# v in two fp16 parts, and gelu and norms in attention with other steps, in an adaLN block of attention and two MLPs

## The chip, the cores and the metric

The kernel runs on one core of one Trainium2 chip. Its time is the device time of one execution in microseconds (us). Before the change the median of three runs is 2027.78 us (2027.35 to 2031.98). A core has engines that work side by side, each through its own instructions in a fixed order: PE (matmul; its weight loads are listed apart as PEld), DVE (vector), ACT (scalar, with functions such as exp and tanh), POOL, and SP, which issues all DMAs here. Matmuls write PSUM, which has 8 banks; POOL works in SBUF only in this kernel.

## The reference, cut to what matters

```python
mod = (silu(c) @ w_mod).reshape(..., 6, 1, -1)
sa, ca, ga, sb, cb, gb = (mod[:, i] for i in range(6))
h = layernorm(x) * (1 + ca) + sa
x = x + ga * attention(h, wqkv, wo)        # 32 heads of 16, softmax over 2048 keys
h = layernorm(x) * (1 + cb) + sb
x = x + gb * mlp(h, w1, w2, w3, w4)

def mlp(x, w1, w2, w3, w4):
    h = gelu(layernorm(x) @ w1)            # tanh form
    hs = shifted(h) @ w2                   # each quarter of the columns moved by +1, -1, +2, -2 rows
    x1 = x + hs
    return x1 + gelu(layernorm(x1) @ w3) @ w4
```

x is 2048 x 512 in fp32, w3 is 512 x 1792. Products other than those with P are made of three matmuls of a high and a low part of each factor.

## The kernel before

Attention goes over 4 chunks of 512 queries and, in each, over 16 pairs of heads: 64 units of 16 steps (128 keys each). A step has two `sc` matmuls (scores, keys by queries, one per head) whose bank ACT turns into P with an exp (L982), and two `mb` matmuls (L970) for a unit that comes later, of which DVE takes the maximum over keys (L966) as the softmax's shift. PE may write a bank again when the exp or the maximum has read it; seven banks are shared by `sc`, `mb` and all other matmuls beside attention, of which those may own three, and one bank holds `pv`.

The exp writes P as an int32 whose upper 16 bits are read as one fp16 number and whose lower 16 bits are the rest. The lower half is turned into fp16 in place, times 0.5, by POOL for a whole step (L1034) or by ACT in two instructions (line 1034's other branch, listed as L123), whichever the planner expects to be done sooner. `pv_part` multiplies both halves with v (L1060 upper half, L1057 lower half). v is kept in DRAM (`Vs`), 192 two-byte numbers per key and pair of heads: three bf16 parts for the upper half, scaled with a constant for the sum of P, and one fp16 part for the lower half. `v_tiles` makes them in chunk 0: two copies on ACT, the rest on DVE, its copy on ACT (L743), the second rest on POOL (L744). After a unit, ACT copies `pv` to `ac` (L1078), PE transposes it, DVE adds the parts (L1096), and POOL divides by the sum.

Beside attention's chunk 0 run the projections and the splitting of weights (`pieces_gen`, with L868 and L869). Beside chunks 1 to 3 run the tails of chunks 0 to 2: wo, the residual, two norms, w1 with gelu, the shift, w2, a norm, w3 with gelu, w4. The rest of the third tail and the whole fourth come after attention, with all 8 banks. A norm's first step in `tail` runs on DVE: centred and times `cbrow` (L1319), times the deviation's inverse plus `sbrow` (L1322). A gelu (`gelu`) beside attention is a chain: ACT square (L1352) and copy (L1353) of the bank, DVE cube (L1357), which frees the bank, ACT tanh (L1361), ACT halving (L1362), POOL product (L1363), ACT high part (L1347), POOL low part (L1348). After attention it is: ACT halved copy (L1366) and square (L1340), which frees the bank, then cube (L1367), tanh (L1368), product (L1369, on DVE), high and low part.

The order is made when the program is built. A planner (`Sched`) keeps a time for each engine by assumed costs; chains wait in a list, and `misc` puts their next step into an engine's order where it expects it not to delay attention's own. `fill` puts matmuls of the projections and tails between blocks of three rows of `sc` and `mb`, with a budget for each step (`SC0`, `TAILB`). The chip then runs each engine in that order and waits on semaphores.

Of the kernel before, what the change touches and what calls it, by code (L numbers as in the profile page):

```python
# [33 lines left out]
VHI = 2.0 ** 39  # L34
VMAX = 2.0 ** 14
VD = 20

SC0 = (32, 900.0, 700.0)
TAILB = (0.0, 500.0, 500.0, 540.0)
# [245 lines left out]
def cA(n=CH):  # L285
    return n / 1.2 + 52
# [11 lines left out]
def kernel(ctx, tc, A_x, A_wqkv, A_wo, B_w1, B_w2, B_w3, B_w4, c, w_mod, out):  # L298
# [45 lines left out]
    def v_hi(t):  # L344
        return t[:, :, 0:128].rearrange("p a (b n) -> p a b n", b=2)
# [205 lines left out]
    def bounds():  # L551
        yield lambda: ("mod", 0) in done and ("mod", 1) in done

        def g():
            dve.scalar_tensor_tensor(gcol, modcol, -1.0, modcol, op0=OP.mult, op1=OP.max)
            dve.scalar_tensor_tensor(gcol[:, 0:4], gcol[:, 4:8], D ** 0.5, gcol[:, 0:4], op0=OP.mult, op1=OP.add)
            dve.tensor_scalar(gcol[:, 0:4], gcol[:, 0:4], 1.0 / (VMAX * VHI), None, op0=OP.mult)
        sch.chain(("D", 250, g), mark("gb"))
# [148 lines left out]
    def v_tiles(w, a, kts):  # L707
        wh, wl = halves(w, KT)
        for kt in kts:
# [13 lines left out]
            r = qp.tile([P, H // 4, 2, DH], F32, name="vr", tag="vr", bufs=2)  # L723

            def rest(v=v, b3=b3, r=r, b=b):
                dve.tensor_tensor(r, b3, v[:, :, :, 0:DH], op=OP.subtract)
# [13 lines left out]
            sch.chain(("A", cA(256), lambda v=v, b3=b3: act.activation(v[:, :, :, 0:DH], b3, AF.Copy)),  # L740
                      ("A", cA(256), lambda vl=vl, b3=b3: act.activation(vl[:, :, :, 8:8 + DH], b3, AF.Copy, scale=1.0 / VHI)),
                      ("D", cD(256), rest),
                      ("A", cA(256), lambda v=v, r=r: act.activation(v[:, :, :, VD:VD + DH], r, AF.Copy)),  # L743
                      ("G", cG(256), lambda v=v, r=r: pool.tensor_tensor(v[:, :, :, 2 * VD:2 * VD + DH], r, v[:, :, :, VD:VD + DH],  # L744
                                                                         op=OP.subtract)),
                      (None, 0, store), prio=VP, bank=b)

    def v_weights(a):
# [94 lines left out]
    def pieces_gen():  # L843
        while True:
# [23 lines left out]
            sch.chain(*ops, ("A", cA(), lambda f=f, w=w: act.activation(w, f, AF.Copy)),  # L868
                      ("G", cG(), lambda f=f, t=t, w=w: pool.tensor_tensor(t, f, w, op=OP.subtract)),  # L869
# [152 lines left out]
    def p_low(s):  # L1022

        p = pt[s].rearrange("p j n -> p (j n)")
        o, i = p.bitcast(F16)[:, 0::2], p.bitcast(U16)[:, 0::2]
        ready = e_exp.pop(s) + XX
        g, a = [max(sch.T[e], ready) for e in "GA"]
        if g > a + LACT:

            for h in range(2):  # L1030
                c = slice(h * CH, (h + 1) * CH)
                e_low[s] = XP["A"] + sch.crit("A", 690, ready, partial(act.activation, o[:, c], i[:, c], AF.Copy, scale=0.5))
        else:
            e_low[s] = XP["G"] + sch.crit("G", 1345, ready, lambda: pool.tensor_scalar(  # L1034
                o, i, 0.5, 1.0, op0=OP.mult, op1=OP.mult))
# [5 lines left out]
    def pv_part(s, lo):  # L1041
# [8 lines left out]
        def mms():  # L1050
            for j in range(2):
                for i in range(2):
                    r = 64 * j + 32 * i
                    if lo:
                        n = 9 + DH if i else 1 + DH
                        c = 128 + 32 * j + 9 + DH
                        te.matmul(acc[r:r + n, :], v[:, (kt + i) % 4, c - n:c].bitcast(F16), pt[s + i].bitcast(F16)[:, j, 0::2],  # L1057
                                  start=False, stop=kt == NKT - 2, skip_group_check=True)
                    else:
                        te.matmul(acc[r:r + 32, :], v[:, kt % 4, r:r + 32], pt[s].bitcast(F16)[:, j, 1::2],  # L1060
# [21 lines left out]
    def o_fin(u, ac, ready):  # L1082
# [12 lines left out]
        def sums():  # L1095
            dve.reduce_sum(sm, bv[:, :, 0:3 * VD].rearrange("p th (a d) -> p th d a", a=3)[:, :, 0:DH + 1, :], axis=AX.X)  # L1096
# [9 lines left out]
        sch.chain(("D", 490, sums), ("D", 90, lambda: dve.reciprocal(rc, sm[:, :, DH:DH + 1])), ("G", 350, fin),  # L1106
# [86 lines left out]
    def tail(ci):  # L1193
# [107 lines left out]
        for i, t in enumerate(new):  # L1301
# [13 lines left out]
            r, m, ops = ln_ops(x1, True)  # L1315
# [8 lines left out]
            go = partial(sch.chain, ("D", cD(), x1_add), ops[0], ("D", cD(), center), ops[1], ("D", cD(), scale), *ops2,  # L1324
# [9 lines left out]
        def gelu(b, n, hi, lo, key):  # L1334
# [4 lines left out]
            def square():  # L1339
                act.activation(sq, b, AF.Square)  # L1340
                sch.free(b)

            def end():
# [3 lines left out]
            tail_ops = (("A", cA(n), lambda: act.activation(hi, xs, AF.Copy)),  # L1347
                        ("G", cG(n), lambda: pool.tensor_tensor(lo, xs, hi, op=OP.subtract)), (None, 0, end))  # L1348
            if psd["s"]:

                def square_copy():
                    act.activation(sq, b, AF.Square)  # L1352
                    act.activation(xs, b, AF.Copy)  # L1353
                    sch.T["A"] += cA(n)

                def cube():
                    dve.scalar_tensor_tensor(sq, sq, 1.0 / GELU_A, b, op0=OP.add, op1=OP.mult)  # L1357
                    sch.free(b)

                sch.chain(("A", cA(n), square_copy), ("D", cD(n), cube),  # L1360
                          ("A", cA(n), lambda: act.activation(sq, sq, AF.Tanh, scale=GELU_A * GELU_C)),  # L1361
                          ("A", cA(n), lambda: act.activation(sq, sq, AF.Copy, scale=0.5, bias=0.5)),  # L1362
                          ("G", cG(n), lambda: pool.tensor_tensor(xs, xs, sq, op=OP.mult)), *tail_ops, bank=b)  # L1363
                return

            sch.chain(("A", cA(n), lambda: act.activation(xs, b, AF.Copy, scale=0.5)), ("A", cA(n), square),  # L1366
                      ("D", cD(n), lambda: dve.scalar_tensor_tensor(sq, sq, 1.0 / GELU_A, xs, op0=OP.add, op1=OP.mult)),  # L1367
                      ("A", cA(n), lambda: act.activation(sq, sq, AF.Tanh, scale=2.0 * GELU_A * GELU_C)),  # L1368
                      ("D", cD(n), lambda: dve.scalar_tensor_tensor(xs, sq, 1.0, xs, op0=OP.add, op1=OP.mult)),  # L1369
                      *tail_ops, bank=b)  # L1370
# [242 lines left out]
```

## Time and profile before

| | |
|---|---|
| median of three runs | 2027.78 us |
| profiled execution | 2035.15 us |
| its span, first to last instruction | 2033.4 us |
| granted PE clock, mean | 0.98 |
| first `sc` matmul | 100.1 us |
| end of attention's chunk 0 | 556.5 us |
| last copy out of `pv` | 1861.3 us |
| exps (L982) | 2048, 1084.1 us busy |
| maxima (L966) | 2048, 1275.7 us busy |
| lower halves of P on POOL (L1034) | 973, 1294.3 us busy |

A group's row names line, engine, operation, tile written and tile read, sizes and count; behind the bar its busy time in us and the mean duration in ns; behind the next bar the idle time of its engine just before its instructions, and what ended that idle time. A row of waits names who waited, for whom, the total in us, how many times, and the longest. PE's busy time holds the whole way of a matmul through the array, so a busy PE is not always one that takes new columns.

### The profile page before, as it was taken

To read this page: it belongs to the slowest core of one execution; us is meant where nothing else is said; L and a number is where in the kernel's file an instruction comes from. 1 tells how busy PE (TensorE), PEld (TensorE's weight loads), DVE (VectorE), ACT (ScalarE), POOL (GpSimd) and SP (SyncE) were. 2 spreads that over 40 slices of the span, in tenths; PEclk is the share of its full clock that TensorE was granted. 3 is DMA by queue.
4 is the path that set the end of the run, shared out by engine and by line. 5 is a ranking of instruction groups with operands and counts; after the bars stand their busy time and mean duration, and the time that the engine had idled before them with its cause. 6 is when DMAs were issued, how large, how long until landed. Compare 5 with 4: busy or idle time off the path is not lost.

```text
span 2033.4 us, 41682 instructions
## 1 busy us (share of the span) xinstructions
PE 1931.8 (95%) x14464; PEld 1151.1 (57%) x14464; DVE 1638.4 (81%) x2936; ACT 1528.8 (75%) x3332; POOL 1700.9 (84%) x1653
## 2 busy tenths in 40 slices
PE   6989999999999999999989999999999999999899
PEld 4655555555454555555445555555555555556788
DVE  8879887687899888788998888788898888872644
ACT  5366887778867987787869897787778888796443
POOL 5378899889988998999889998898889998897532
PEclk8999999999998999999999999999999999999899
DMA  5664578876643334434523433333533233434332
GB/s 188 193 199 145 169 215 248 267 230 229 194 146 113 113 109 128 128 119 149 156 86 92 133 113 109 102 118 122 161 109 106 88 113 113 154 93 153 150 125 89
DMA packets 230619, 293.20 MB, mean 144 GB/s; under 512 B 123636, under 2 KB 175348, under 8 KB 214120
## 3 DMA queue, kind: packets, MB, share of 16 engines
q1 hardware_dynamic: 230408, 290.53, 45.5%
q8 instruction: 115, 1.88, 0.4%
q14 instruction: 96, 0.79, 0.1%
HBM read 226.49 MB, written 62.91 MB: 142 GB/s over the span
## 4 chain that ended last, share of the span: by engine, by line
PE 58%; DVE 16%; ACT 14%; POOL 5%; DMA 3%; issue 3%; SPq 1%; POOLq 0%; DVEq 0%; ACTq 0%
PE mb L970 12%; DVE mx L966 9%; PE pv L1060 9%; PE sc L986 8%; ACT pt L982 8%; PE w L326 6%; PE w L328 5%; PE w L330 5%; PE pv L1057 4%; POOL pt L1034 3%; ACT pt L123 1%; PE ot L1089 1%; SPq L102 1%; ACT sq L1352 1%; DVE tst L337 1%
## 5 line engine op out<-in xcount | busy, mean ns | idle before, releaser
L1034 POOL TENSOR_SCALAR pt<-pt 128x1024 f16<-128x1024 uint16 x973 | 1294.3, 1367 | 117.3 <-ACT pt L982 114.9
L966 DVE TENSOR_REDUCE mx<-mb 128x1 f32<-128x512 f32 x2048 | 1275.7, 682 | 112.5 <-PE mb L970 87.1
L982 ACT ACTIVATE pt<-sc 128x512 int32<-128x512 f32 x2048 | 1084.1, 614 | 235.1 <-PE mb L970 185.5
L970 PE MATMUL mb<-kst,qtl 64*128 64x512 f32 x2048 | 758.0, 454 | 56.0 <-ACT pt L982 23.2
L986 PE MATMUL sc<-qtl,kst 64*128 64x512 f32 x2048 | 721.2, 445 | 7.5 <-ACT pt L982 1.8
L970 PEld LDWEIGHTS mb<-kst,qtl 64*128 64x128 f32 x2048 | 348.9, 193 | 266.0 <-ACT pt L982 101.2
L986 PEld LDWEIGHTS sc<-qtl,kst 64*128 64x128 f32 x2048 | 335.6, 186 | 163.5 <-DVE mx L966 49.4
L1060 PE MATMUL pv<-pt,vst 128*32 128x512 f16 x4096 | 360.0, 399 | 3.2 <-DMA vst<-Vs 3.2
L1057 PE MATMUL pv<-pt,vst 128*17 128x512 f16 (+1 forms) x2048 | 211.6, 394 | 1.8 <-POOL pt L1034 1.3
L1060 PEld LDWEIGHTS <-vst 128*32 128x32 bf16 x4096 | 91.3, 95 | 168.8 <-issue 107.7
L326 PE MATMUL w<-A,wr 128*128 128x256 f32 (+2 forms) x576 | 177.6, 308 | 1.6 <-ACT A L320 1.4
L1348 POOL TENSOR_TENSOR g<-xs,g 128x256 fp32r<-128x256 f32 (+2 forms) x144 | 104.2, 724 | 84.9 <-ACT g L1347 84.8
L328 PE MATMUL w<-A,wr 128*128 128x256 f32 (+2 forms) x576 | 170.8, 297 | 1.0 <-DVE A L316 0.7
L330 PE MATMUL w<-A,wr 128*128 128x256 f32 (+2 forms) x576 | 168.9, 293 | 0.0
L326 PEld LDWEIGHTS w<-A,wr 128*128 128x128 f32 x576 | 111.2, 193 | 33.2 <-DVE mx L966 11.2
L326 PE MATMUL w<-wr,g 128*128 128x512 f32 x288 | 118.9, 413 | 0.9 <-ACT g L1347 0.9
L328 PEld LDWEIGHTS w<-A,wr 128*128 128x128 f32 x576 | 111.4, 193 | 12.8 <-issue 10.5
L330 PEld LDWEIGHTS w<-A,wr 128*128 128x128 f32 x576 | 111.4, 193 | 6.5 <-issue 6.5
L330 PE MATMUL w<-wr,g 128*128 128x512 f32 x288 | 113.7, 395 | 0.3 <-POOL g L1348 0.3
L328 PE MATMUL w<-wr,g 128*128 128x512 f32 x288 | 113.6, 395 | 0.0
L1450 DVE TENSOR_TENSOR x<-x,w 128x512 f32<-128x512 f32 x64 | 44.0, 687 | 84.5 <-PE w L330 84.2
L1357 DVE SCALAR_TENSOR_TENSOR sq<-sq,w 128x256 f32<-128x256 f32 (+1 forms) x108 | 43.3, 401 | 64.5 <-ACT xs L1353 60.4
(148 smaller groups left out, 2250.7 us busy)
## 6 DMA issues: line engine op xcount, KB each, us to landing
wr<-Ws SPq DMA_DIRECT2D x80, 1024.0 KB
vst<-Vs SPq DMA_DIRECT2D x256, 192.0 KB
kst<-Ks SPq DMA_DIRECT2D x189, 256.0 KB
qtl<-Qs SPq DMA_DIRECT2D x192, 64.0 KB
Vs<-vt SPq DMA_DIRECT2D x32, 384.0 KB
Ws<-wq SPq DMA_DIRECT2D x40, 256.0 KB
Ws<-wst SPq DMA_DIRECT2D x40, 256.0 KB
wst<-in_B_w_dram SPq DMA_DIRECT2D x36, 256.0 KB
```

The lines of the kernel that those rows point to most:

```text
L326: te.matmul(o, lh, rh, start=first, stop=False)
L328: te.matmul(o, lh, rl, start=False, stop=False)
L330: te.matmul(o, ll, rh, start=False, stop=last)
L966: end = sch.crit("D", 605, e + PX, lambda: dve.reduce_max(mxs[u][:, j, g, c:c + 1], b, axis=AX.X))
L970: return ready, lambda: te.matmul(b, lhs, kst[u % 3][r, c * CH:(c + 1) * CH], start=True, stop=True), after
L982: ea = sch.crit("A", 480, e + PX, lambda: act.activation(pt[s][:, j], b, AF.Exp))
L986: return ready, lambda: te.matmul(b, kst[u % 3][r, kt * P:(kt + 1) * P], qst[u][r], start=True, stop=True), after
L1034: e_low[s] = XP["G"] + sch.crit("G", 1345, ready, lambda: pool.tensor_scalar(o, i, 0.5, 1.0, op0=OP.mult, op1=OP.mult))
L1057: te.matmul(acc[r:r + n, :], v[:, (kt + i) % 4, c - n:c].bitcast(F16), pt[s + i].bitcast(F16)[:, j, 0::2], start=False, stop=kt == NKT - 2 ...
L1060: te.matmul(acc[r:r + 32, :], v[:, kt % 4, r:r + 32], pt[s].bitcast(F16)[:, j, 1::2], start=kt == 0, stop=False, skip_group_check=True)
L1348: ("G", cG(n), lambda: pool.tensor_tensor(lo, xs, hi, op=OP.subtract)), (None, 0, end))
L1450: dve.tensor_tensor(x1, x1, b, op=OP.add)
```

## The change

- v is kept as two fp16 parts for the upper half of P, and one fp16 part, scaled, for the lower half. The third part's two steps (L743, L744) go; DVE writes the second part itself. The ones that make the sum of P change their constant, and the lower half of P is multiplied by 2^-22 instead of 0.5. DVE adds two parts instead of three (136 x 2 numbers instead of 136 x 3). All lower-half matmuls have 17 columns of weights, of which half had 25. `Vs` keeps its size.
- A gelu has one form in all places: ACT square, DVE cube, ACT tanh, DVE product, ACT high part, POOL low part. Cube and product both read the bank, which is free after the product. The factor 0.5 goes into w2 and w4 (18 ACT instructions when they are split).
- Four norms in each of the first three tails go another way: ACT applies mean and deviation (L1281), POOL multiplies with `cbrow` and adds `sbrow` (L1330, L1331).
- Nine of the 40 low parts of split weights go from POOL to DVE (in pieces of wo and w4).
- `TAILB`, the planner's budget of filling work per step, is 560 in the third and fourth chunk instead of 500 and 540.

```diff
-VHI = 2.0 ** 39
-VMAX = 2.0 ** 14
-VD = 20
+VMAX = 2.0 ** 15
+VONE = 2.0 ** 8
+PLOW = 2.0 ** -22
+VLOW = 2.0 ** -40 / PLOW
...
-TAILB = (0.0, 500.0, 500.0, 540.0)
+TAILB = (0.0, 500.0, 560.0, 560.0)
...
             def rest(v=v, b3=b3, r=r, b=b):
-                dve.tensor_tensor(r, b3, v[:, :, :, 0:DH], op=OP.subtract)
+                dve.tensor_tensor(v[:, :, :, 1, 0:DH], b3, v[:, :, :, 0, 0:DH], op=OP.subtract)
                 sch.free(b)
...
                       ("D", cD(256), rest),
-                      ("A", cA(256), lambda v=v, r=r: act.activation(v[:, :, :, VD:VD + DH], r, AF.Copy)),
-                      ("G", cG(256), lambda v=v, r=r: pool.tensor_tensor(v[:, :, :, 2 * VD:2 * VD + DH], r, v[:, :, :, VD:VD + DH],
-                                                                         op=OP.subtract)),
                       (None, 0, store), prio=VP, bank=b)
...
+            if nm in ("w2", "w4"):
+                ops.append(("A", cA(), lambda f=f: act.activation(f, f, AF.Copy, scale=0.5)))
             sch.chain(*ops, ("A", cA(), lambda f=f, w=w: act.activation(w, f, AF.Copy)),
+                      ("D", 2 * cD(), lambda f=f, t=t, w=w: dve.tensor_tensor(t, f, w, op=OP.subtract)) if nm in rows and c else
                       ("G", cG(), lambda f=f, t=t, w=w: pool.tensor_tensor(t, f, w, op=OP.subtract)),
...
             e_low[s] = XP["G"] + sch.crit("G", 1345, ready, lambda: pool.tensor_scalar(
-                o, i, 0.5, 1.0, op0=OP.mult, op1=OP.mult))
+                o, i, PLOW, 1.0, op0=OP.mult, op1=OP.mult))
...
-            dve.reduce_sum(sm, bv[:, :, 0:3 * VD].rearrange("p th (a d) -> p th d a", a=3)[:, :, 0:DH + 1, :], axis=AX.X)
+            dve.reduce_sum(sm, bv.rearrange("p th (a d) -> p th d a", a=2)[:, :, 0:DH + 1, :], axis=AX.X)
...
-            r, m, ops = ln_ops(x1, True)
+            way = not end and i in (0, 1, 2, 3)
+            if way:
+                r, ops = ln_ops(x1)
+                m = None
+            else:
+                r, m, ops = ln_ops(x1, True)
...
+            if way:
+                norm = (*ops, ln_apply(xb, x1, r), ("G", cG(), lambda xb=xb: pool.tensor_tensor(xb, xb, cbrow, op=OP.mult)),
+                        ("G", cG(), lambda xb=xb: pool.tensor_tensor(xb, xb, sbrow, op=OP.add)))
+            else:
+                norm = (ops[0], ("D", cD(), center), ops[1], ("D", cD(), scale))
...
+            def cube():
+                dve.scalar_tensor_tensor(sq, sq, 1.0 / GELU_A, b, op0=OP.add, op1=OP.mult)
+
+            def prod():
+                dve.scalar_tensor_tensor(xs, sq, 1.0, b, op0=OP.add, op1=OP.mult)
+                sch.free(b)
+
+            sch.chain(("A", cA(n), lambda: act.activation(sq, b, AF.Square)), ("D", cD(n), cube),
+                      ("A", cA(n), lambda: act.activation(sq, sq, AF.Tanh, scale=GELU_A * GELU_C)),
+                      ("D", cD(n), prod),
+                      ("A", cA(n), lambda: act.activation(hi, xs, AF.Copy)),
+                      ("G", cG(n), lambda: pool.tensor_tensor(lo, xs, hi, op=OP.subtract)), (None, 0, end), bank=b)
```

The planner makes a new order from it. The built programs count: lower halves of P on POOL 973 before and 999 now, ACT instructions for them 102 and 50 (70 and 38 while the planner is in chunks 1 to 3, 30 and 12 in chunk 0). PE has 14384 matmuls in both; 854 stand after the last `pv` matmul before, 869 now.

Three places show how the order moves. The first is ACT in the tail of chunk 0, a gelu of w1 (`w_10733` before, `w_10579` now, is its bank; `pt<-sc` rows are exps). Before:

```order
L1352 ACTIVATE sq<-w_10733 128x256
L1353 ACTIVATE xs<-w_10733 128x256
L982 ACTIVATE pt_612<-sc 128x512
L982 ACTIVATE pt_613<-sc 128x512 x2
L1361 ACTIVATE sq<-sq 128x256
L1362 ACTIVATE sq<-sq 128x256
L982 ACTIVATE pt_614<-sc 128x512 x2
L982 ACTIVATE pt_615<-sc 128x512 x2
L982 ACTIVATE pt_608<-sc 128x512 x2
L1347 ACTIVATE g_10732<-xs 128x256
```

Now, up to the same high part:

```order
L1360 ACTIVATE sq<-w_10579 128x256
L982 ACTIVATE pt_602<-sc 128x512
L982 ACTIVATE pt_603<-sc 128x512 x2
L1361 ACTIVATE sq<-sq 128x256
L1078 ACTIVATE ac<-pv 128x512
L982 ACTIVATE pt_604<-sc 128x512 x2
L1363 ACTIVATE g_10578<-xs 128x256
```

The copy behind the square and the halving behind the tanh are gone, and the high part comes after two exps instead of six.

The second place is DVE at the same gelu; `mx<-mb` rows are maxima. Before:

```order
L966 TENSOR_REDUCE mx<-mb 128x1 x7
L1357 SCALAR_TENSOR_TENSOR sq<-sq,w_10733 128x256
L966 TENSOR_REDUCE mx<-mb 128x1 x8
L1016 TENSOR_REDUCE mf<-mx 128x8
L966 TENSOR_REDUCE mx<-mb 128x1 x3
```

Now, with the next gelu's two rows behind it:

```order
L1354 SCALAR_TENSOR_TENSOR sq<-sq,w_10579 128x256
L966 TENSOR_REDUCE mx<-mb 128x1 x2
L1357 SCALAR_TENSOR_TENSOR xs<-sq,w_10579 128x256
L966 TENSOR_REDUCE mx<-mb 128x1 x4
L1354 SCALAR_TENSOR_TENSOR sq<-sq,w_10703 128x256
L966 TENSOR_REDUCE mx<-mb 128x1 x2
L1357 SCALAR_TENSOR_TENSOR xs<-sq,w_10703 128x256
```

The product (now L1357) stands two maxima behind its cube (now L1354), as it does in 87 of the 108 gelus beside attention.

The third place is POOL at the first norms of the first tail; `pt<-pt` rows are lower halves of P, `trs` rows the deviation's inverse and what is made of it, one column each. Before:

```order
L1034 TENSOR_SCALAR pt_611<-pt_611 128x1024
L1270 TENSOR_TENSOR trs<-tmv,mhalf 128x1
L1034 TENSOR_SCALAR pt_612<-pt_612 128x1024
L1034 TENSOR_SCALAR pt_613<-pt_613 128x1024
L1034 TENSOR_SCALAR pt_614<-pt_614 128x1024
```

Now:

```order
L1270 TENSOR_TENSOR trs<-tmv,mhalf 128x1
L1274 TENSOR_TENSOR trs<-tmv,trs 128x1
L1275 TENSOR_SCALAR trs<-trs 128x1
L1034 TENSOR_SCALAR pt_604<-pt_604 128x1024
L1330 TENSOR_TENSOR xb<-xb,cbrow 128x512
L1331 TENSOR_TENSOR xb<-xb,sbrow 128x512
L1034 TENSOR_SCALAR pt_605<-pt_605 128x1024
```

Two products over 512 columns stand between two lower halves of P, and two more one-column steps behind the first.

More of the change, by code (lines that the diff above doesn't have):

```diff
@@ L344, in v_hi @@
     def v_hi(t):
[L345 removed]
+        return t[:, :, 0:128].bitcast(F16).rearrange("p a (b i n) -> p a b i n", b=2, i=2)
     def v_lo(t):
@@ L1104, in fin @@
                 sch.add(tail(ci))
-        sch.chain(("D", 490, sums), ("D", 90, lambda: dve.reciprocal(rc, sm[:, :, DH:DH + 1])), ("G", 350, fin),
+        sch.chain(("D", 350, sums), ("D", 90, lambda: dve.reciprocal(rc, sm[:, :, DH:DH + 1])), ("G", 350, fin),
                   *([mark(("att", ci))] if pr == NP - 1 else []), prio=0, bank=b)
@@ L1345, in end @@
                 live.remove(key)
[L1347 to L1370, printed above, removed]
+            def cube():
[8 more added lines that the diff above has]
+                      ("G", cG(n), lambda: pool.tensor_tensor(lo, xs, hi, op=OP.subtract)), (None, 0, end), bank=b)
         def wait_bank():
```

30 lines of the change are left out of this document (13 added, 17 removed).

## The prediction

> **What bounds the kernel now.** I read the page's busy shares and chain first, then the window view cut where the trace shows the first score matmul (100.1), the end of attention's first chunk (556.5) and the last copy out of `pv` (1861.3).
>
> ```profile
> PE 1931.8 (95%) x14464; PEld 1151.1 (57%) x14464; DVE 1638.4 (81%) x2936; ACT 1528.8 (75%) x3332; POOL 1700.9 (84%) x1653
> ...
> PE 58%; DVE 16%; ACT 14%; POOL 5%; DMA 3%; issue 3%; SPq 1%; POOLq 0%; DVEq 0%; ACTq 0%
> ```
> ```profile
> core 0: us, PE busy (x) PEld busy (x) DVE busy (x) ACT busy (x) POOL busy (x), PEclk, DMA share, GB/s
> 0.00:100.10 100.10, 80.27 (x371) 56.41 (x371) 81.13 (x160) 42.78 (x83) 45.41 (x62) 0.90 0.60 188
> 100.10:556.50 456.40, 434.73 (x3267) 243.71 (x3267) 366.22 (x638) 352.66 (x728) 409.45 (x351) 0.97 0.69 211
> 556.50:1861.30 1304.80, 1259.30 (x9981) 712.70 (x9980) 1099.49 (x1967) 1059.27 (x2341) 1184.48 (x1154) 0.99 0.38 118
> 1861.30:2033.40 172.10, 157.53 (x851) 138.23 (x849) 91.56 (x172) 74.13 (x182) 61.56 (x89) 0.96 0.37 137
> ```
>
> Call the four stretches A, B (chunk 0, with the v and q/k projections beside it), C (chunks 1 to 3, with three tails) and D (the rest). In C no engine is alone the bound: PE is busy 97%, POOL 91%, DVE 84%, ACT 81%, all in fixed orders that wait on each other. The groups of C show who holds PE:
>
> ```profile
> L1034 POOL TENSOR_SCALAR pt<-pt 128x1024 f16<-128x1024 uint16 x736 | 978.8, 1366 | 86.4 <-ACT pt L982 84.6
> L966 DVE TENSOR_REDUCE mx<-mb 128x1 f32<-128x512 f32 x1490 | 928.9, 682 | 64.3 <-PE mb L970 51.5 <-PE sc L986 7.9
> L982 ACT ACTIVATE pt<-sc 128x512 int32<-128x512 f32 x1538 | 816.5, 615 | 190.8 <-PE mb L970 149.9 <-PE sc L986 36.8 <-POOL pt L1034 1.7
> L970 PE MATMUL mb<-kst,qtl 64*128 64x512 f32 x1489 | 549.0, 451 | 39.9 <-ACT pt L982 16.6 <-DVE mx L966 6.1 <-DVE sq L1357 5.8
> ...
> L970 PEld LDWEIGHTS mb<-kst,qtl 64*128 64x128 f32 x1488 | 254.2, 193 | 187.8 <-ACT pt L982 72.4 <-DVE mx L966 51.3 <-issue 15.3
> ...
> L986 PEld LDWEIGHTS sc<-qtl,kst 64*128 64x128 f32 x1536 | 249.3, 185 | 118.6 <-ACT pt L982 34.9 <-DVE mx L966 32.6 <-issue 18.2
> ```
>
> PE waits 72.4 + 34.9 + 16.6 = 123.9 us for exps that free a bank, and 51.3 + 32.6 = 83.9 us for maxima that do. A weight load's wait is not all lost, since earlier matmuls still run: before the `mb` matmuls PE itself idles 39.9 us where their loads idle 187.8, 21%. That ratio and 1 are the two ends below.
>
> **The change, stretch C.** 106 of the 108 gelus of the run that stand in attention are here.
>
> ```profile
> L1363 POOL TENSOR_TENSOR xs<-xs,sq 128x256 f32<-128x256 f32 (+1 forms) x108 | 76.1, 705 | 12.7 <-ACT sq L1362 11.7
> ...
> L1362 ACT ACTIVATE sq<-sq 128x256 f32<-128x256 f32 (+1 forms) x108 | 46.8, 433 | 1.6
> ...
> L1357 DVE SCALAR_TENSOR_TENSOR sq<-sq,w 128x256 f32<-128x256 f32 (+1 forms) x108 | 43.3, 401 | 64.5 <-ACT xs L1353 60.4 <-POOL pt L1034 3.7 <-POOL trs L1270 0.2
> ...
> L1353 ACT ACTIVATE xs<-w 128x256 f32<-128x256 f32 (+1 forms) x108 | 41.8, 387 | 0.0
> ```
> ```profile
> L123 ACT ACTIVATE pt<-pt 128x512 f16<-128x512 uint16 x72 | 51.9, 808 | 0.0
> ...
> L1418 POOL TENSOR_TENSOR xb<-xb,gbrow 128x512 f32<-128x512 f32 x11 | 14.2, 1293 | 0.0
> ...
> L1322 DVE SCALAR_TENSOR_TENSOR xb<-xb,trs,sbrow 128x512 f32<-128x512 f32 x12 | 12.9, 1073 | 0.0
> ...
> L1319 DVE SCALAR_TENSOR_TENSOR xb<-x,tmv,cbrow 128x512 f32<-128x512 f32 x12 | 10.4, 864 | 0.0
> ```
> ```profile
> L1281 ACT ACTIVATE xn<-xb,trs 128x512 f32<-128x512 f32 x32 | 26.2, 818 | 29.3 <-POOL trs L1275 29.3
> ...
> L1275 POOL TENSOR_SCALAR trs<-trs 128x1 f32<-128x1 f32 x32 | 6.6, 207 | 2.8
> ...
> L1096 DVE TENSOR_REDUCE sm<-ot 128x136 f32<-128x408 f32 x64 | 36.8, 575 | 5.8 <-PE ot L1089 5.8
> ```
>
> - ACT loses the copy (41.0 us for 106) and the halving (45.9). By the changed order 34 of the 72 half-P conversions leave it (51.9 / 72 = 0.72 us, 24.5). It gains 12 norm applies like L1281 (9.8). Sum **-101.6 us**. ACT's work beside the exps is 1059.3 - 816.5 = 242.8, so 42% of it goes.
> - DVE gains a second product per gelu, which reads the bank as L1357 does: +42.5. It loses 12 norms' two steps (-23.3) and a third of the elements in 48 sums (at most 192 ns each; I take 7 us in all). Sum **+12**, 7% of its 170.6 us beside the maxima.
> - POOL loses L1363 (-74), gains 17 conversions of 1.33 us (978.8 / 736; +22.6), 24 products like L1418 (+31) and 24 one-column steps (+5). Sum **-15**.
> - PE's instruction counts stay. The parts of v are fp16 instead of bf16, stationary at 32 columns for the upper half of P and 17 (half of them 25 before) for the lower; I price that at nothing, since the bf16 and the fp16 kind differ by 1% here:
>
> ```profile
> L1060 PE MATMUL pv<-pt,vst 128*32 128x512 f16 x4096 | 360.0, 399 | 3.2 <-DMA vst<-Vs 3.2
> ...
> L1057 PE MATMUL pv<-pt,vst 128*17 128x512 f16 (+1 forms) x2048 | 211.6, 394 | 1.8 <-POOL pt L1034 1.3
> ```
>
> The new product's price hangs on its operands. In D the cube reads a copy in SBUF, and so does the product:
>
> ```profile
> L1369 DVE SCALAR_TENSOR_TENSOR xs<-sq,xs 128x256 f32<-128x256 f32 x22 | 12.6, 571 | 10.4 <-ACT sq L1368 9.9 <-POOL g L1348 0.6
> ...
> L1322 DVE SCALAR_TENSOR_TENSOR xb<-xb,trs,sbrow 128x512 f32<-128x512 f32 x4 | 3.0, 743 | 0.0
> ```
>
> With two SBUF operands the product takes 571 ns, with one in the bank 401 (L1357, some of its tiles smaller); and the same norm step takes 743 ns in D but 1073 in C, where POOL is busier. I take 401 and keep 571 as the upper end, +18 us of DVE. [...]
>
> **From engine time to span in C.** If PE's waits for exps shrink with what ACT does besides, 42% of 123.9 is -52 us. Waits for DVE grow, with these rows:
>
> ```profile
> DVE sq L1357 <- ACT xs L1353: 56.5, 63, 6.8
> ...
> PEld w L326 <- DVE mx L966: 16.7, 44, 0.5
> ...
> PEld mb L970 <- DVE sq L1357: 13.0, 19, 1.2
> ```
>
> 7% of 83.9 + 16.7 is +7, and a second DVE step per gelu doubles the 13.0. That leaves -32 if all of it is lost time, -7 at the 21%; the middle is -19. A wait goes and one comes: the cube no longer waits out ACT's copy (0.39 us, 63 times, -24 us of DVE idling), but the product waits for the tanh, with the maxima queued behind it, which free PE's banks. The new order puts two maxima (1.36 us) between cube and product; a tanh is about as long as the removed L1362 (0.43). So the new wait lies between 0 and the old 56.5; I let the two nearly cancel and take -3. C: **-22**.
>
> **Stretch B.**
>
> ```profile
> L982 ACT ACTIVATE pt<-sc 128x512 int32<-128x512 f32 x510 | 267.6, 612 | 44.3 <-PE mb L970 35.6 <-PE sc L986 5.5 <-POOL pt L1034 2.6
> ...
> L970 PEld LDWEIGHTS mb<-kst,qtl 64*128 64x128 f32 x513 | 89.2, 194 | 71.1 <-ACT pt L982 28.8 <-DVE mx L966 21.7 <-issue 5.5
> ...
> L869 POOL TENSOR_TENSOR wst<-wst,wq 128x512 fp32r<-128x512 f32 x40 | 51.8, 1301 | 3.9 <-ACT wq L868 3.9
> ...
> L868 ACT ACTIVATE wq<-wst 128x512 fp32r<-128x512 f32 x40 | 25.8, 644 | 6.8 <-POOL wst L857 3.8 <-DMA Ws<-wq 3.0
> ...
> L744 POOL TENSOR_TENSOR vt<-vr,vt 128x256 bf16<-128x256 f32 x22 | 16.1, 737 | 13.1 <-ACT vt L743 13.1
> ...
> L426 DVE TENSOR_TENSOR wp<-wst,wp 128x512 fp32r<-128x512 f32 x10 | 10.6, 1067 | 0.0
> ...
> L743 ACT ACTIVATE vt<-vr 128x256 bf16<-128x256 f32 x21 | 9.3, 451 | 1.6 <-DVE vr L726 1.6
> ```
>
> ACT: -9.3, 18 conversions fewer (30 to 12 in the order, -13), 18 halvings of w2 and w4 more (+11.6): -11, 13% of its 85 us beside the exps. DVE: nine weight remainders from POOL, at L426's 1.07 us +10, sums -2. POOL: -16.1 - 11.7 + 9 x 1.33 = -16, while it is the busiest at 90%. The PE waits that ACT frees (13% of 28.8) and those that DVE adds are under 5 us each and cancel; the end set by POOL is -16 / 0.9 = -18, the other end +6. I take **-3**.
>
> **Stretches A and D.** Ten of the 32 v tiles (L744 has 22 in B) fall into A, where their two removed steps run beside PE's projections and the store to `Vs` keeps its size: 0; the end is the 10 x 0.73 us of POOL work, -7. D's order has 15 matmuls more behind the last `pv` (869 for 854); at 157.53 / 851 = 0.185 us, +2.8. That is also all that the larger `TAILB` budgets amount to in the end, and they shift filling matmuls between the steps of C only. In D the gelu loses its copy:
>
> ```profile
> L1366 ACT ACTIVATE xs<-w 128x256 f32<-128x256 f32 (+1 forms) x36 | 15.0, 417 | 43.4 <-PE w L330 42.6 <-POOL g L1348 0.5
> ```
>
> ACT is idle more than half of D and PE stops only 14.6 us, so I give -1.8 of the 15.0. D: **+1**. Together -22 - 3 + 1 = **-24 us**. The profiled execution took 2035.15 (span 2033.4 and 1.75 around it), 7.4 above the median of the three runs, so I subtract from both alike: 2011 profiled, **2004** as median.
>
> **Rivals.**
> - PE is the bound, and ACT only idles more. For: 97% busy, and exps already wait 149.9 us for `mb`. Against: those waits end where banks are freed by ACT. Price: the 21% end, -7 in C, 0 in B, +1 to +2.8 in D: about -5, 2023.
> - All the freed time counts. C -32 with DVE's -24 added in part, B -18: about -50, 1978. For: POOL, the fullest but PE, loses work as well. Against: DVE gains 12.
> - Slower: the product stalls DVE at its place behind the tanh, and maxima behind it keep banks from PE. If it waits like the cube did (56.5 / 63 = 0.9 us) on half to all of 106, that is 48 to 95 us; half of it lost at PE, less the 24 gained, is 0 to +24 (2028 to 2052); from a mean wait of 0.45 us on all of them nothing is left of the gain. The bank, which the gelu holds until the product, is late at the same place. For: the product sits in DVE's fixed order, and PE already waits 13.0 us behind the cube. Against: ACT, which makes the tanh late, has 102 us less to do. I price it at 2050.
> - POOL, with 17 conversions more and the norms, stalls `pv`: its sum is still -15, so I fold this into the first.
>
> **Chances.** Forecast (1988 to 2016) 0.49; deeper 0.15; PE-bound (2016 to 2034) 0.20; slower 0.16. A measurement tells from no change about 0.3%, 6 us. Faster takes the first two and 0.06 of the third: 0.70; same 0.13; slower 0.17. The range 1976 to 2038 takes in all but 0.05 below and 0.13 above.
>
> **What would show it.** Right: in C, ACT near 958 busy, DVE near 1110, POOL near 1170, the weight loads' waits for `pt` L982 well under 107 us, C some 1283 long. Wrong: DVE's product idling over 45 us behind the tanh; or PE's waits for ACT gone and C as long, which is the PE-bound case; or D longer than 175.

## The result and the profile after

| | before | after |
|---|---|---|
| median of five runs, us | 2027.78 (2026.82 to 2032.26) | 2080.09 (2074.76 to 2081.40) |
| profiled execution: span, us | 2033.4 | 2078.3 |
| granted PE clock, mean | 0.98 | 0.98 |

The changed kernel takes 1.0233 times as long (95% interval 1.0218 to 1.0248), some 47 us more by that ratio (the medians of the table differ by 52), where the prediction had 24 less. The page of the changed kernel, busy shares and then the chain by engine and by line:

```profile
PE 1941.8 (93%) x14464; PEld 1156.6 (56%) x14464; DVE 1646.4 (79%) x3029; ACT 1452.2 (70%) x3026; POOL 1726.5 (83%) x1578
...
PE 53%; POOL 17%; DVE 14%; ACT 7%; issue 4%; DMA 3%; SPq 1%; POOLq 0%; ACTq 0%; DVEq 0%
POOL pt L1034 13%; PE mb L970 11%; DVE mx L966 8%; PE sc L986 8%; PE pv L1060 7%; PE w L327 6%; PE w L331 5%; PE w L329 5%; ACT pt L982 4%; PE pv L1057 4%; DMA vst<-Vs 1%; SPq L103 1%; PE ot L1089 1%; DVE sq L1354 1%; DVE xs L1357 1%
```

ACT's share of the chain fell from 14% to 7%. But POOL's rose from 5% to 17%, and 13% is one line: L1034, the conversion of the lower half of P. The busy share of POOL does not show it, 83% after 84%.

The window view of the changed kernel, cut at the same events as in the prediction (first `sc` matmul 99.8, end of chunk 0 562.7, last copy out of `pv` 1904.9), with the same columns:

```profile
0.00:99.80 99.80, 78.54 (x392) 56.88 (x392) 81.43 (x161) 40.06 (x77) 38.12 (x51) 0.91 0.63 193
99.80:562.70 462.90, 432.90 (x3249) 241.70 (x3248) 369.70 (x645) 341.71 (x699) 407.07 (x324) 0.97 0.66 203
562.70:1904.90 1342.20, 1272.62 (x9962) 719.00 (x9959) 1109.18 (x2047) 1006.15 (x2108) 1221.99 (x1118) 0.98 0.37 117
1904.90:2078.30 173.40, 157.75 (x869) 139.02 (x869) 86.07 (x178) 64.33 (x146) 59.31 (x86) 0.97 0.36 135
```

Against before A is 0.3 us shorter, B 6.5 longer, C 37.4 longer and D 1.3 longer: 44.9 in the span, nearly all of it where POOL converts P. DVE (1109) is where the prediction had it (near 1110); POOL is 52 us over its 1170.

How a group tells this apart from more work. The row of all conversions, first of the kernel before, then of the changed one with the matmuls that read what it writes:

```profile
L1034 POOL TENSOR_SCALAR pt<-pt 128x1024 f16<-128x1024 uint16 x973 | 1294.3, 1367 | 117.3 <-ACT pt L982 114.9
```
```profile
L1034 POOL TENSOR_SCALAR pt<-pt 128x1024 f16<-128x1024 uint16 x999 | 1360.3, 1362 | 146.1 <-ACT pt L982 70.0
...
L1057 PE MATMUL pv<-pt,vst 128*17 128x512 f16 x2048 | 227.1, 394 | 28.2 <-POOL pt L1034 27.7
```

One conversion lasts as long as before (1362 and 1367 ns). But 973 times 1367 ns is 1330 us and the busy time 1294: the conversions lay over each other or over a neighbour by 36 us. 999 times 1362 ns is 1360.6, the busy time to 0.3 us: now nothing overlaps. And of the idle time ahead of a conversion all but 2.4 us had a releaser before; now 146.1 - 70.0 = 76 us have none, 76 ns for each. They are gaps of about 79 ns, one ahead of most conversions, too short for the rows to name what ended them. The matmuls behind it, which stood 1.3 us for L1034, stand 27.7.

The timeline shows the seams themselves (start, duration; a row of x3 is three in a run). The kernel before:

```profile
999.14 3.92 POOL L1034 TENSOR_SCALAR pt<-pt 128x1024 f16<-128x1024 uint16 x3
...
1003.17 1.33 POOL L1034 TENSOR_SCALAR pt<-pt 128x1024 f16<-128x1024 uint16 x1
1004.45 0.39 POOL L1100 TENSOR_TENSOR osb<-sm,rc 128x128 f32<-128x128 f32 x1
```

The changed kernel, some 25 us later:

```profile
1027.90 1.35 POOL L1034 TENSOR_SCALAR pt<-pt 128x1024 f16<-128x1024 uint16 x1
1029.33 0.20 POOL L1019 TENSOR_TENSOR nm<-mf,nm 128x8 fp32r<-128x8 f32 x1
1029.49 0.41 POOL L1100 TENSOR_TENSOR osb<-sm,rc 128x128 f32<-128x128 f32 x1
1029.98 9.93 POOL L1034 TENSOR_SCALAR pt<-pt 128x1024 f16<-128x1024 uint16 x7
```

Before, L1100 starts at 1004.45 while the conversion ahead of it runs to 1004.50. After, L1019 starts 0.08 us behind a conversion's end (1027.90 + 1.35 = 1029.25), and the next conversion 0.08 behind L1100's end; between L1019 and L1100 there is an overlap as ever (0.04 us). Three conversions in a run took 3.92 us, one each (3.92 - 1.36) / 2 = 1.28; seven now take 9.93, one each 1.43. Over the whole traces the median from start to start of two conversions that follow directly, less than 1.7 us apart, is 1289 ns (522 pairs) and 1437 ns (640 pairs): **148 ns more each**, with their duration unchanged. What changed in this instruction is one number: the factor, 0.5 before and 2^-22 now.

### The profile page after: what moved, and what is told of

Same layout as the page of the kernel before. It is cut to its first block, busy times and chain, and to the rows that moved or that the text cites. A ratio compares the mean times of both kernels' runs of the same rounds, so it can differ in the third digit from the quotient of the medians.

```text
span 2078.3 us, 42310 instructions
## 1 busy us (share of the span) xinstructions
PE 1941.8 (93%) x14464; PEld 1156.6 (56%) x14464; DVE 1646.4 (79%) x3029; ACT 1452.2 (70%) x3026; POOL 1726.5 (83%) x1578
## 4 chain that ended last, share of the span: by engine, by line
PE 53%; POOL 17%; DVE 14%; ACT 7%; issue 4%; DMA 3%; SPq 1%; POOLq 0%; ACTq 0%; DVEq 0%
POOL pt L1034 13%; PE mb L970 11%; DVE mx L966 8%; PE sc L986 8%; PE pv L1060 7%; PE w L327 6%; PE w L331 5%; PE w L329 5%; ACT pt L982 4%; PE pv L1057 4%; DMA vst<-Vs 1%; SPq L103 1%; PE ot L1089 1%; DVE sq L1354 1%; DVE xs L1357 1%
## 5 line engine op out<-in xcount | busy, mean ns | idle before, releaser
L1034 POOL TENSOR_SCALAR pt<-pt 128x1024 f16<-128x1024 uint16 x999 | 1360.3, 1362 | 146.1 <-ACT pt L982 70.0
L1057 PE MATMUL pv<-pt,vst 128*17 128x512 f16 x2048 | 227.1, 394 | 28.2 <-POOL pt L1034 27.7
L1060 PEld LDWEIGHTS <-vst 128*32 128x32 f16 x4096 | 91.5, 95 | 173.3 <-issue 110.5
L327 PE MATMUL w<-A,wr 128*128 128x256 f32 (+2 forms) x576 | 176.2, 306 | 0.3 <-ACT A L321 0.3
L327 PEld LDWEIGHTS w<-A,wr 128*128 128x128 f32 x576 | 110.0, 191 | 34.2 <-issue 10.5
L327 PE MATMUL w<-wr,g 128*128 128x512 f32 x288 | 119.2, 414 | 1.9 <-DVE xs L1357 1.9
L1057 PEld LDWEIGHTS <-vst 128*17 128x17 f16 x2048 | 59.6, 90 | 97.0 <-issue 54.2
```

The source lines that it names most:

```text
L327: te.matmul(o, lh, rh, start=first, stop=False)
L1057: te.matmul(acc[r:r + n, :], v[:, (kt + i) % 4, c:c + n].bitcast(F16), pt[s + i].bitcast(F16)[:, j, 0::2], start=False, stop=kt == NKT - 2 ...
L1060: te.matmul(acc[r:r + 32, :], v[:, kt % 4, r:r + 32].bitcast(F16), pt[s].bitcast(F16)[:, j, 1::2], start=kt == 0, stop=False, skip_group_c ...
```

## The experiments

"Apart" below means that conversions stand 79 ns behind the end of the one ahead, "overlapped" that they start about 70 ns before it. Ratios are to the kernel before, run on the same chip; its medians there were 2029.7 to 2031.2 us.

**Is it the factor at all?** The changed kernel with the old factor, and the kernel before with the new one:

```diff
 e1_pool_half (changed kernel)
-                o, i, PLOW, 1.0, op0=OP.mult, op1=OP.mult))
+                o, i, 0.5, 1.0, op0=OP.mult, op1=OP.mult))
 e2_before_small (kernel before)
-                o, i, 0.5, 1.0, op0=OP.mult, op1=OP.mult))
+                o, i, 2.0 ** -22, 1.0, op0=OP.mult, op1=OP.mult))
```

> The kernel after, but POOL multiplies the lower halves of P by 0.5 as before, not by 2^-22 (ACT's fifty keep 2^-22), so the lower halves that POOL makes are weighted wrongly; the order of all instructions is that of the kernel after. Theory T1 (the new scale costs POOL time: in the kernel after seven conversions in a row take 9.93 us, before 9.27 us, and each starts some 80 ns behind the end of the one ahead instead of 70 ns ahead of it): seven in a row are back at 9.1 to 9.3 us, POOL's busy time per conversion back from 1.362 to 1.33 us, PE's wait of 27.7 us for L1034 at its lower-half matmuls falls under 8 us, and the time falls to 2000 to 2025. Rival T2 (POOL is late because of its load and place in the order, 26 conversions and 24 norm products more): spacing and time stay, 2074 to 2086.

Measured: 2018.49 us, ratio 0.9937 (0.9915 to 0.9959); start to start 1291 ns. One number in one instruction takes back all of the loss and 13 us more.

> The kernel before, with POOL multiplying the lower halves of P by 2^-22 instead of 0.5 (ACT's part keeps 0.5), so the lower halves that POOL makes are weighted wrongly; nothing else changes. T1: each of the 973 conversions costs about 0.15 us more of POOL from start to start, and as POOL was busy 84% and up to 97% in some stretches, the time rises by 40 to 110 us, to 2070 to 2140. T2: 2028 within 6 us.

Measured: 2117.02 us, ratio 1.0411 (1.0379 to 1.0442); start to start 1435 ns. Its row of conversions and its timeline:

```profile
L1034 POOL TENSOR_SCALAR pt<-pt 128x1024 f16<-128x1024 uint16 x973 | 1323.3, 1360 | 131.3 <-ACT pt L982 57.0
```
```profile
1035.76 4.21 POOL L1034 TENSOR_SCALAR pt<-pt 128x1024 f16<-128x1024 uint16 x3 [0.56 <-ACT pt L982]
...
1044.00 1.34 POOL L1034 TENSOR_SCALAR pt<-pt 128x1024 f16<-128x1024 uint16 x1
1045.42 0.40 POOL L1100 TENSOR_TENSOR osb<-sm,rc 128x128 f32<-128x128 f32 x1
```

The signs are those of the changed kernel: 973 times 1360 is 1323.3, no overlap; 74 us of idle time have no releaser; three in a run take 4.21 us instead of 3.92; L1100 starts 0.08 us behind a conversion. So the factor does it in either kernel, and by more in the kernel before; its POOL has more to do besides, but that this is the reason is not shown. Everything else in the change together is a gain of under 1% (e1 here, e3 below).

**The same results with other numbers, or results of another kind.** By arithmetic the product of the two factors decides what is written; the factors themselves stand in the instruction. e3 splits 2^-22 in two equal factors, which by arithmetic gives the same values. e4 takes a factor with which no result is subnormal in fp16.

```diff
 e3_two_factors
-                o, i, PLOW, 1.0, op0=OP.mult, op1=OP.mult))
+                o, i, 2.0 ** -11, 2.0 ** -11, op0=OP.mult, op1=OP.mult))
 e4_no_subnormals
-                o, i, PLOW, 1.0, op0=OP.mult, op1=OP.mult))
+                o, i, 2.0 ** -14, 1.0, op0=OP.mult, op1=OP.mult))
```

> The kernel after, with the two factors of POOL's conversion 2^-11 and 2^-11 instead of 2^-22 and 1: the same results. Variant T1a (what counts is the number that stands in the instruction, very small against 0.5): conversions are close again as before, seven in a row 9.1 to 9.3 us, 2000 to 2025. Variant T1b (what counts are the results: most are fp16 numbers, those under 2^-14 subnormal) and T2: 2074 to 2086.

Measured: **2016.00 us, ratio 0.9921 (0.9900 to 0.9942)**, overlapped (1290 ns). It writes the same values as the changed kernel and beats both kernels.

> The kernel after, with POOL's factor 2^-14, so that no result is a subnormal fp16 number (whole numbers times 2^-14); the lower halves are weighted wrongly. T1b: close conversions, 2000 to 2025. T1a with any number but 0.5 slow, and T2: 2074 to 2086. T1a with very small numbers alone slow: between the two.

Measured: 2076.26 us, ratio 1.0223 (1.0201 to 1.0245), apart (1435 ns). The rows of the two, e3 first:

```profile
L1034 POOL TENSOR_SCALAR pt<-pt 128x1024 f16<-128x1024 uint16 x999 | 1327.2, 1365 | 142.3 <-ACT pt L982 138.6 <-POOL pt L1034 0.5 <-POOL nm L1019 0.2
```
```profile
L1034 POOL TENSOR_SCALAR pt<-pt 128x1024 f16<-128x1024 uint16 x999 | 1359.2, 1361 | 150.0 <-ACT pt L982 74.1
```

The theory that subnormal results make POOL slower falls twice: e3 writes the same ones and overlaps, e4 has none and stands apart. It is the number in the instruction, not the values that come out.

**Which numbers?** Left were: a factor too small, the second factor or its place, or some pattern in the number's bits. Four more pairs; e5 and e6 change `PLOW`, and `VLOW` with it; e7 and e8 keep the product at 2^-22.

```diff
 e5_low_m23
-PLOW = 2.0 ** -22
+PLOW = 2.0 ** -23
 e6_low_m21
-PLOW = 2.0 ** -22
+PLOW = 2.0 ** -21
 e7_m6_m16
-                o, i, PLOW, 1.0, op0=OP.mult, op1=OP.mult))
+                o, i, 2.0 ** -6, 2.0 ** -16, op0=OP.mult, op1=OP.mult))
 e8_one_first
-                o, i, PLOW, 1.0, op0=OP.mult, op1=OP.mult))
+                o, i, 1.0, PLOW, op0=OP.mult, op1=OP.mult))
```

> The kernel after with the lower halves scaled by 2^-23 in place of 2^-22 (v's part for them follows: PLOW alone is changed). First factors seen so far: 0.5 and 2^-11 close (fast), 2^-14 and 2^-22 apart (slow). Theory Tm (size: a first factor below some bound between 2^-11 and 2^-14 is slow): seven conversions in a row take 9.9 us, 2074 to 2086. Theory Tb (bits: the biased fp32 exponents of the slow ones, 113 and 105, are 1 modulo 4, those of the fast ones, 126 and 116, are 2 and 0): 2^-23 has 104, so conversions are close, 9.1 to 9.3 us, 2010 to 2022.

> The same with 2^-21 (exponent 106, 2 modulo 4). Tm: slow, 2074 to 2086. Tb: close, 2010 to 2022.

> The kernel after with POOL's two factors 2^-6 and 2^-16, the same results. Tm: the first factor is large, so close, 2010 to 2022. Tb: its exponent is 121, 1 modulo 4, so slow, 2074 to 2086 (2^-16 has 111, 3 modulo 4).

> The kernel after with POOL's two factors in the other order, 1 and then 2^-22, the same results. If only the first factor counts, close under Tm and under Tb (1 has 127, 3 modulo 4): 2010 to 2022. If the second counts too, slow under both: 2074 to 2086.

Measured: e5 2018.40 us, ratio 0.9948 (0.9931 to 0.9966), overlapped (1289 ns). e6, e7 and e8, one run each: 2075.83, 2083.08 and 2073.65 us, all apart (1435 to 1436 ns). The rows of e5 and e6 read like e3's and e4's:

```profile
L1034 POOL TENSOR_SCALAR pt<-pt 128x1024 f16<-128x1024 uint16 x999 | 1327.5, 1367 | 143.6 <-ACT pt L982 139.7 <-POOL pt L1034 0.5 <-POOL nm L1019 0.2
```
```profile
L1034 POOL TENSOR_SCALAR pt<-pt 128x1024 f16<-128x1024 uint16 x999 | 1358.7, 1360 | 146.0 <-ACT pt L982 70.0
```

A smaller factor (e5) overlaps and a larger one (e6) does not, so size is out. In e8 the small factor stands second and 1 first, and it stays apart, so its place is out. What is left is a pattern in the exponent. By the exponent field of fp32 (the power plus 127), 2^-23 and 2^-11 have 104 and 116, multiples of 4. Those that stood apart have 105 (2^-22), 113 (2^-14), 106 (2^-21), and in e7 121 and 111: none of them a multiple of 4. The pattern as it was expected before these four runs, that only fields that are 1 modulo 4 are slow, fell with e6 (106 is 2 modulo 4). So the rule was fitted to seven pairs after they were seen, and e6 alone, in one run, tells a multiple of 4 from any even field. e9 tests it on two numbers that had not been used:

```diff
 e9_m7_m15
-                o, i, PLOW, 1.0, op0=OP.mult, op1=OP.mult))
+                o, i, 2.0 ** -7, 2.0 ** -15, op0=OP.mult, op1=OP.mult))
```

> The kernel after with POOL's two factors 2^-7 and 2^-15, the same results. Theory Tq (the two low bits of a factor's fp32 exponent decide: fast so far are pairs of 0.5, 1 and numbers with exponent 0 modulo 4, namely 104 and 116; every pair with another number, 105, 106, 113, 121 with 111, was slow): 120 and 112 are both 0 modulo 4, so close, 2010 to 2022. Rival (the fast ones share something else, such as being small or equal): slow, 2072 to 2086.

Measured, one run: 2021.84 us, overlapped (1290 ns), with exponent fields 120 and 112. The rule holds in all eight pairs with a small factor, of which e9 alone was forecast by it; 0.5 and 1 (126 and 127) overlap with each other and are exceptions that it doesn't explain.

| first, second factor | exponent fields | start to start, ns |
|---|---|---|
| 0.5, 1 | 126, 127 | 1288 to 1291 |
| 2^-11, 2^-11 | 116, 116 | 1290 |
| 2^-23, 1 | 104, 127 | 1289 |
| 2^-7, 2^-15 | 120, 112 | 1290 |
| 2^-22, 1 | 105, 127 | 1435 to 1437 |
| 2^-21, 1 | 106, 127 | 1435 |
| 2^-14, 1 | 113, 127 | 1435 |
| 2^-6, 2^-16 | 121, 111 | 1436 |
| 1, 2^-22 | 127, 105 | 1435 |

**What the rest of the change is worth, part by part.** e3 is the change without the factor's cost. From it, one kernel puts the four norms back on DVE; one gives the gelu its form of before, everywhere, and leaves w2 and w4 unhalved; and one makes the planner favour ACT for conversions. In each the planner makes a new order, with its own split of conversions (999 on POOL in e3, 1008 in p1).

```diff
 p1_norms_back (from e3)
-            way = not end and i in (0, 1, 2, 3)
+            way = False
 p3_gelu_back (from e3; the gelu of before, both forms)
-            if nm in ("w2", "w4"):
-                ops.append(("A", cA(), lambda f=f: act.activation(f, f, AF.Copy, scale=0.5)))
...
-                      ("D", cD(n), prod),
...
+                sch.chain(("A", cA(n), square_copy), ("D", cD(n), cube),
...
+                          ("G", cG(n), lambda: pool.tensor_tensor(xs, xs, sq, op=OP.mult)), *tail_ops, bank=b)
 p4_more_on_act (from e3)
-LACT = 800.0
+LACT = 0.0
```

> The kernel e3_two_factors (2016) with the twelve norms in attention back on DVE: POOL loses 24 products of 1.29 us and some small steps (-36 us), ACT 12 applies (-10), DVE gains 24 steps (+23). If POOL is what bounds the chunks now, it is faster, 1996 to 2010. If DVE's maxima are, slower, 2022 to 2035. If the two balance, within 6 us of 2016.

> The kernel e3_two_factors with the gelu of the kernel before, beside attention and after it, and w2 and w4 not halved: ACT gets 87 us of copies and halvings back in the chunks, POOL 74 us of products, DVE loses 42 us. By the prediction's sum the gelu carries most of the gain: 2028 to 2045. Rival (the gain comes from v's two parts and the norms): 2010 to 2022.

> The kernel e3_two_factors with the planner sending a lower half of P to ACT as soon as POOL is later than ACT (LACT 0 in place of 800): 102 ACT instructions for it in place of 50, so POOL loses 26 conversions (about -34 us), ACT gains 37 us. If POOL's lateness still holds the chunks: 2000 to 2012. If not, 2012 to 2024.

Measured: p1 2029.83 us, ratio 0.9999 (0.9989 to 1.0008); p3 2032.98, ratio 1.0013 (1.0003 to 1.0022); p4 2020.41, ratio 0.9951 (0.9934 to 0.9968). The four stretches of e3, then C of p1 and of p3, in the window view:

```profile
0.00:98.20 98.20, 78.94 (x390) 56.99 (x390) 81.37 (x161) 40.20 (x77) 38.09 (x51) 0.91 0.64 197
98.20:549.50 451.30, 430.73 (x3247) 239.66 (x3248) 370.77 (x645) 340.97 (x699) 394.68 (x325) 0.97 0.67 207
549.50:1841.00 1291.50, 1252.95 (x9962) 710.87 (x9958) 1107.42 (x2047) 1003.49 (x2107) 1171.76 (x1117) 0.99 0.38 122
1841.00:2014.20 173.20, 158.62 (x869) 140.53 (x869) 86.22 (x178) 64.38 (x146) 59.24 (x86) 0.96 0.36 136
```
```profile
549.30:1861.50 1312.20, 1270.69 (x10004) 722.44 (x10002) 1130.06 (x2080) 991.85 (x2089) 1160.20 (x1082) 0.98 0.38 121
```
```profile
549.30:1855.00 1305.70, 1256.20 (x9966) 709.69 (x9963) 1073.98 (x1942) 1081.36 (x2371) 1199.61 (x1191) 0.99 0.38 120
```

Each time the slowest of the forecast ranges came true. Neither half pays without the other. With the new gelu and the old norms (p1), DVE has 1130 us to do, 31 more than before, and C is 7 us longer than before. With the old gelu and the new norms (p3), POOL has 1200 and ACT 1081, both more than before, and C is 1 us longer. Together none of the three is above 1172 and C is 13 us shorter. Both kernels keep v's two parts and the rest of the change; what these are worth alone was not tried. p4 moves 26 more conversions to ACT (973 are left on POOL for 999, 52 more ACT instructions) and gains nothing over e3: its C is 1285.9 us long, 5.6 shorter, but its chunk 0 466.7, 15.4 longer. Whether the shift in C alone would keep the 5.6 was not tried.

## Why the prediction was wrong

**The step that failed** is the one on POOL: "gains 17 conversions of 1.33 us (978.8 / 736; +22.6)", in a sum of -15. It priced every conversion, the other 736 too, at what one took with the factor 0.5; the new factor itself has no line in the sum. The 1.33 us from busy time by count already held the overlap as if it were a property of the shape. With 2^-22 it was gone, for all 999. The conversions of C, first of the changed kernel, then of e3:

```profile
L1034 POOL TENSOR_SCALAR pt<-pt 128x1024 f16<-128x1024 uint16 x753 | 1022.9, 1358 | 88.6 <-ACT pt L982 30.2
```
```profile
L1034 POOL TENSOR_SCALAR pt<-pt 128x1024 f16<-128x1024 uint16 x753 | 996.9, 1361 | 85.9 <-ACT pt L982 83.8 <-POOL pt L1034 0.3 <-POOL nm L1019 0.2
```

The count is the forecast one (736 + 17). With overlap they take 18 us more than the 978.8 of before, for the 22.6 of the forecast. With 2^-22 they take 44 more than before, and 58 us of short gaps stand ahead of them besides (2 before): some 100 us where the term said 22.6.

How 148 ns each become the loss, from the rows. From e3 to the changed kernel the instructions are the same (42310 on both pages); only the factors differ. POOL's busy time on the page goes from 1663.8 to 1726.5, +62.7; the idle time ahead of conversions that no releaser explains goes from 3 to 76 us, +73. So POOL is taken up 136 us longer. Its waits for exps shrink from 138.6 to 70.0, which takes up 69 of them. That leaves 67 us, and the span grows by 2078.3 - 2014.2 = 64. The page of e3, for its busy shares and its chain:

```profile
PE 1921.2 (95%) x14464; PEld 1148.0 (57%) x14464; DVE 1645.8 (82%) x3029; ACT 1449.0 (72%) x3026; POOL 1663.8 (83%) x1578
...
PE 69%; DVE 15%; ACT 7%; POOL 4%; DMA 3%; issue 3%; SPq 1%; POOLq 0%; ACTq 0%; DVEq 0%
```

**The rival that came nearest** is the last, "POOL, with 17 conversions more and the norms, stalls `pv`", which had been folded into the first because POOL's sum was negative. Its outcome is what the trace shows (27.7 us of `pv` waiting for L1034, POOL 17% of the chain against e3's 4%). Its cause is not: e3 has the same conversions and norms, and there `pv` waits for next to nothing:

```profile
L1057 PE MATMUL pv<-pt,vst 128*17 128x512 f16 x2048 | 211.0, 394 | 0.2
```

The factor was in no rival. The range ended at 2038, and the profile of before could not have given 2080; but the number was new in an instruction that runs 999 times, and a bound for it was owed.

**The rest of the forecast**, read from e3, where the factor costs nothing: A -1.9 (0 forecast), B -5.1 (-3), C -13.3 (-22), D +1.1 (+1); together -19.2 of -24. The profiled execution of before is 7 us above its median, so part of this is spread: by its ratio e3 gains 16 us.

- DVE's and POOL's sums in C were right where the factor costs nothing: 1107 against "near 1110", 1172 against "near 1170".
- ACT's was not: 1003 against "near 958". 55.8 us went, not 101.6. Summed over all of ACT's groups in C, busy time does fall by 109 us (1177.9 to 1068.7); but the groups lie over each other, by 119 us before and 65 in e3, so the engine's own busy time falls by half of that. The timeline of ACT before shows a gelu's square and copy:

```profile
756.20 0.39 ACT L1352 ACTIVATE sq<-w 128x256 f32<-128x256 f32 x1
756.48 0.38 ACT L1353 ACTIVATE xs<-w 128x256 f32<-128x256 f32 x1
756.75 1.58 ACT L982 ACTIVATE pt<-sc 128x512 int32<-128x512 f32 x3
```

The copy lasts 0.38 us, but the exp starts 0.27 after it: taking the copy out gives 0.27. The prediction took durations. In C of the kernel before, the median overlap of two ACT instructions that lie over each other is 120 ns (1912 pairs), and the 92 copies of 256 columns (L1353, 402 ns each) start a median of 264 ns ahead of what follows. At the 0.11 us of the rows above, the 234 instructions that are gone make an estimated 26 us, about half of what is missing; besides, fewer of those left stand close, with 1553 overlapping pairs in C of e3 after 1912.

- So PE's waits for exps shrank less. The groups of C in e3:

```profile
L970 PE MATMUL mb<-kst,qtl 64*128 64x512 f32 x1489 | 544.1, 451 | 32.8 <-ACT pt L982 11.8 <-DVE xs L1357 8.1 <-DVE mx L966 4.8
...
L970 PEld LDWEIGHTS mb<-kst,qtl 64*128 64x128 f32 x1487 | 252.9, 192 | 178.7 <-DVE mx L966 64.1 <-ACT pt L982 51.9 <-DVE xs L1357 13.4
L986 PEld LDWEIGHTS sc<-qtl,kst 64*128 64x128 f32 x1535 | 250.0, 185 | 114.1 <-DVE mx L966 34.3 <-issue 25.8 <-ACT pt L982 25.1
```

Waits for exps are 51.9 + 25.1 + 11.8 = 88.8 us, 35 less than the 123.9 of before and not 52 less; those of the weight loads for maxima 64.1 + 34.3 = 98.4, 14.5 more than 83.9. The same halving as in the prediction, between all of it and 21%, gives (35 - 14.5) x 0.6 = 12, and C lost 13.3. The prediction's other waits moved too: those of L326 (now L327) for maxima fell from 16.7 to 13.0 us, where they were to grow, those behind the gelu's DVE step stood at 13.4 after 13.0, where they were to double, and L327's for exps rose from 2.4 to 12.2. Over all of PE's waits for ACT and DVE in C the sum falls by as much, from 316 to 295 us. So e3 agrees with the mechanism of C, with ACT's term sized too large; the 0.6 was not measured.

- The product, in the changed kernel's groups of C:

```profile
L1354 DVE SCALAR_TENSOR_TENSOR sq<-sq,w 128x256 f32<-128x256 f32 x90 | 37.4, 416 | 27.0 <-ACT sq L1360 26.4
...
L1357 DVE SCALAR_TENSOR_TENSOR xs<-sq,w 128x256 f32<-128x256 f32 x90 | 36.9, 410 | 5.8 <-ACT sq L1361 5.8
```

The price of 401 ns holds (410), and the rival "the product stalls DVE behind the tanh" is refuted: 5.8 us of waiting for 90 products (and 3.9 for the 14 smaller ones), where 45 was the sign to look for. The cubes' went from 56.5 to 28.5 (26.4 here, 2.1 for the smaller). The product reads one operand in the bank and takes 410 ns (420 in D of the changed kernel) where two in SBUF took 571 in D of the kernel before.

- "PE is the bound" did not hold either: PE has the same 14464 matmuls in e3, p1 and p3 (the pages of before and after have 14464 as well, not the 14384 of the section on the change), and their C is 1291.5, 1312.2 and 1305.7 us long, with PE idle 39, 42 and 50 us.

**What stays open** is why the chip does it; no run here shows that. POOL's seam depends on a number in the instruction, and the multiple of 4 is a rule found on eight pairs of powers of two, in this one instruction (uint16 to fp16, two multiplications, 1024 columns).

The traces do show seams of the same size elsewhere on POOL. The one-column steps of a norm read what the step ahead of them writes. In e3:

```profile
1013.25 2.65 POOL L1034 TENSOR_SCALAR pt<-pt 128x1024 f16<-128x1024 uint16 x2 [2.56 <-ACT pt L982]
1015.83 0.54 POOL L1270 TENSOR_TENSOR trs<-tmv,mhalf 128x1 f32<-128x1 f32 x1
1016.45 0.19 POOL L1274 TENSOR_TENSOR trs<-tmv,trs 128x1 f32<-128x1 f32 x1
1016.73 0.19 POOL L1275 TENSOR_SCALAR trs<-trs 128x1 f32<-128x1 f32 x1
1016.88 1.37 POOL L1034 TENSOR_SCALAR pt<-pt 128x1024 f16<-128x1024 uint16 x1
```

L1270 starts 0.07 us before the conversion ahead of it ends. But L1274, which reads what L1270 writes, starts 0.08 us behind its end, and L1275 0.09 behind that of L1274; in all 44 such places of e3 the medians are 78 and 88 ns. The seams of the changed kernel are as long: 79 ns between conversions, 80 ns ahead of another instruction behind one. So a conversion with such a factor is spaced as if it had to wait for the end of what stands ahead, and what follows for its own, although e3 has the same program except for the factors and does not wait.

## What to carry to other kernels

- A constant was part of an instruction's price here: 1437 ns from start to start with 2^-22 and 1, 1290 with 2^-11 twice. When a change alters only the immediate of an instruction that runs a thousand times, measure its spacing with the new number; if it must have a given product, try it as two factors. Here one line (2^-11 twice for 2^-22 and 1) turns 1.023 into 0.992.
- In a row of a group compare count times mean with busy time, and the idle time with its releasers. Overlap that vanishes (36 us here) and many short gaps without a releaser (76 us) meant that POOL was taken up longer while its busy share stood still (84%, then 83%). What an instruction in a row of others frees when it goes is its spacing in the timeline (0.27 us for the gelu's copy), not its duration (0.38).
- Two moves that each overload another engine can pay together (p1 1.000, p3 1.001, both 0.992). Test the parts before dropping one, and the whole before keeping it.

## What was not expected of the hardware

- POOL conversions with the factors 0.5 and 1 start about 70 ns before the one ahead ends (median 73 in the kernel before); with 2^-22 and 1 they start 79 ns behind its end, and other instructions behind a conversion 80 ns behind its end. The duration of one (1.36 us) says nothing of it. Size, place and the values that come out do not decide; fp32 exponent fields that are multiples of 4 overlapped in all three pairs tried, and so did 0.5 and 1, which that rule leaves unexplained.
- ACT instructions in a row lay over each other: in C by a median of 120 ns before (1912 pairs) and 112 ns in the changed kernel (1544 pairs). With 234 fewer in C of e3 (2341 to 2107), 109 us by their groups, ACT was busy 56 us less.
